# Two batches turned by the tensor engine, products read from PSUM, and a mixer half that no longer shares its time with attention

## The chip, the cores and the metric

The kernel runs on one core of a Trainium2 chip. The metric is device time in microseconds (us). Five engines work side by side, each through its own instructions in order: TensorE (PE; PEld is its weight load), VectorE (DVE), ScalarE (ACT), GpSimd (POOL), and SyncE (SP), which here issues all DMAs from one queue. A step starts when its inputs have come and the buffer it writes is free. TensorE writes to PSUM; DVE and ACT read PSUM, POOL does not.

## The reference

```python
# q, k, v, f_logit: (4, 8, 768, 48); U (768, 32), V (32, 768), w_ch1 (384, 1536), w_ch2 (1536, 384)
f = 1.0 / (1.0 + np.exp(-f_logit))
for t in range(S):                       # gated linear attention, per batch and head
    state = f[:, :, t, :, None] * state + np.einsum('bhd,bhe->bhde', k[:, :, t], v[:, :, t])
    y[:, :, t] = np.einsum('bhd,bhde->bhe', q[:, :, t], state)
x = y.transpose(0, 2, 1, 3).reshape(4, 768, 384)
h = x.transpose(0, 2, 1) @ U @ V         # low-rank mixing over the sequence
u = x + h.transpose(0, 2, 1)
out = u + np.maximum(u @ w_ch1, 0.0) @ w_ch2
```

All data are f32 on the chip; the weights come as f64 and are turned into f32 there.

## The kernel before

Attention works in 16 units of two heads, four to a batch, numbered 0 to 15. Each batch's mixer follows its attention. Two generators give a unit's pieces. `prepare(n)` makes the operands: `gates` (f to channel-major form, sigmoid), `keep` (a backward scan X, L353), `keys` (k times X), `read` (a forward scan Y, L370), `queries` (q times Y, and then the loads of unit n+2 are issued). `attend(n)` has `kept` (k back to token-major form), `scores` for each half of the six 128-token chunks with a causal mask (L406), `states` (products in `ds`, L426, then a short scan of states `st`, L432 and L437), and `read` (40 matmuls with the states, 48 with the masked scores `A`, into `y`). A loop over units writes `prepare(n + 1)` between the pieces of `attend(n)`.

There are two ways to channel-major form. Batch 0 is loaded token-major, in rows of 48 floats (192 bytes), and TensorE transposes it into PSUM (`pt`, L321); ACT copies k and q out, and POOL multiplies them (L336). The other batches are loaded as overlapping runs of 1136 floats for each of 32 rows, and DVE transposes them in blocks (L302); POOL multiplies too.

The mixer of a batch (`mixer_pieces`) has a first part, `low_rank` (`ph`), `mix` (`pu`, added to x by DVE) and `turn` (`put`, copied to `uT` by ACT). Then for each half of the sequence come 12 `ch1` pieces (`pz`, L147, each with a relu `z` on ACT) and 3 `ch2` pieces (`po`, L156, added to x and stored). A piece of `ch1` needs one third of a column block of w_ch1; each `ch2` piece needs all of w_ch2 and all 12 `z`. `pz`, `po`, `pu`, `put`, `ph` and `ds` share two PSUM buffers; `pt`, `sc` and `y` share three others.

`Fill` spreads the mixer pieces of a batch over the 40 slots of the next batch's attention, by cost; the last three `ch2` pieces of a batch are put around the first part of the next mixer. `ahead_by(2, weights)` makes 27 calls, one for each piece of weight, each of which issues a load two pieces ahead and turns the loaded piece into f32: two steps on ACT (L57, L58), three on DVE (L59 to L61), one on POOL (L62). The raw pieces have three buffers, the intermediate ones two. The first 15 pieces (U, V, w_ch1) are spread over batch 0's attention, the 12 of w_ch2 over batch 0's mixer part.

The order on each engine is set by a scheduler that weighs these pieces; the rows of the order are therefore shown with the change.

Of the kernel before, what the change touches and what calls it, by code (L numbers as in the profile page):

```python
# [9 lines left out]
F32 = mybir.dt.float32  # L10
U32 = mybir.dt.uint32
U64 = mybir.dt.uint64
# [4 lines left out]

WP = 384
PAD = 64

# [7 lines left out]
def weight_loader(nc, pool, dma):  # L28
# [8 lines left out]
    def load(dst, w):  # L37
# [4 lines left out]
        T = {}  # L42

        def start():
            raw = T["raw"] = pool.tile([P, WP], U64, name="w_raw", bufs=3)[0:rows, 0:n]
            if len(dst.shape) == 3:
                raw = raw.rearrange("p (c n) -> p c n", c=dst.shape[1])
            dma.dma_start(out=raw, in_=w)
# [58 lines left out]
def mixer_pieces(nc, b, x, U, V, w1, w2, ident, out, two, three, zp, ps_mm):  # L107
# [11 lines left out]
    def low_rank():  # L119
        pm = ps_mm.tile([P, 512], F32, name="ph", tag="mm")  # L120

        for c in range(NCH):
            g = slice((c % NG) * R, (c % NG + 1) * R)
            nc.tensor.matmul(pm[g, 0:DM], lhsT=U[:, c, :], rhs=x[:, c, :],  # L124
                             start=(c < NG), stop=(c >= NCH - NG))
        h[0] = two.tile([P, DM], F32, name="h")
        nc.scalar.copy(h[0], pm[:, 0:DM])
# [46 lines left out]
def factored_path(ctx, tc, q, k, v, f_logit, moe_U, moe_V, moe_w_ch1, moe_w_ch2, out, ok):  # L174
# [20 lines left out]
    HC = C // 2  # L195

    assert S % (2 * C) == 0 and H % 2 == 0 and NB < D <= PAD and PAD == 2 * NB and S % NB == 0
    assert DM % P == 0 and FF % P == 0 and FF % WP == 0 and DM == WP and DM <= 512 and R % 32 == 0 and P % R == 0 and P // R <= NCH
# [24 lines left out]
    def load_unit(n):  # L223
        b, hp = divmod(n, HP)
        for nm in "fkq":
            if b == 0:
                for par in range(2):
                    nc.sync.dma_start(
                        out=nat[n % 2][nm][:, :, par, 0:D],
                        in_=src[nm][b, 2 * hp + par].rearrange("(c p) d -> p c d", p=C),  # L230
                    )
                continue
# [35 lines left out]
    nc.vector.memset(ends, 0.0)  # L268
    nc.vector.memset(ends.rearrange("p (c t) -> p c t", t=C)[:, :, C - 1], 1.0)
    fz = [const.tile([P, S + 1], F32, name=f"fz{i}") for i in range(2)]  # L270
    starts = [const.tile([P, S], F32, name=f"starts{i}") for i in range(2)]
    for i in range(2):
        nc.gpsimd.memset(fz[i], 0.0)
        nc.gpsimd.memset(starts[i], 0.0)
    least = const.tile([P, NU, NCH], F32, name="least")
# [33 lines left out]
    def prepare(n):  # L309
# [3 lines left out]
        b = n // HP  # L313
        r, f, e = raw[n % 2], fz[n % 2], starts[n % 2]
        by_chunk = f[:, 0:S].rearrange("p (c t) -> p c t", t=C)
# [14 lines left out]
        def operand(nm, of):  # L330
            t = T[nm] = two.tile([P, S], F32, name=f"{nm}T")
            if b == 0:
                nc.scalar.copy(halves(t), on_tensor(nm))
            else:
                turned(t, r[nm])
            nc.gpsimd.tensor_tensor(t, t, T[of], ALU.mult)  # L336

        def gates():
            f0 = T["f0"] = two.tile([P, NCH], F32, name="f0")
            if b == 0:  # L340
                pt = on_tensor("f")
                nc.scalar.activation(halves(f)[:, :, :, 1:C], pt[:, :, :, 1:C], AF.Sigmoid)
                nc.scalar.activation(f0.rearrange("p (a c) -> p a c", a=2), pt[:, :, :, 0], AF.Sigmoid)
                return
# [6 lines left out]
        def keep():  # L351
# [5 lines left out]
            X0 = X.rearrange("p (c t) -> p c t", t=C)[:, :, 0]  # L357
            nc.vector.tensor_copy(least[:, n, :], X0)
            X1 = two.tile([P, NCH], F32, name="X1")
            nc.vector.tensor_single_scalar(X1, X0, LEAST, ALU.max)  # L360
            nc.vector.reciprocal(e.rearrange("p (c t) -> p c t", t=C)[:, :, 0], X1)
            whole = T["whole"] = two.tile([P, NCH], F32, name="whole")
# [5 lines left out]
        def read():  # L368
            Y = T["Y"] = one.tile([P, S], F32, name="Y")
            nc.vector.tensor_tensor_scan(Y, f[:, 0:S], e, 0.0, ALU.mult, ALU.add)  # L370

# [12 lines left out]
    def attend(n):  # L384
# [7 lines left out]
        def scores(g):  # L392
# [4 lines left out]
            for c in range(G):  # L397
                for par in range(2):
# [5 lines left out]
                    )  # L404
            for par in range(2):
                nc.vector.tensor_tensor(  # L406
                    T["A"][:, par, g * G : (g + 1) * G, :],
                    sc[:, par, 0 : G * C].rearrange("p (c i) -> p c i", i=C),
                    causal.unsqueeze(1).broadcast_to((P, G, C)),
                    ALU.mult,  # L410
                )

# [64 lines left out]
    load_unit(1)  # L477
    loads = ahead_by(2, weights)
    todo = [(1, f) for f in loads[:first]]
    for piece in prepare(0):  # L480
        piece()
    after = []
    for b in range(B):
# [13 lines left out]
        if b == 0:  # L497

            todo = before + main[0:NFC]
            for i, f in enumerate(loads[first:]):  # L500
                todo.insert(2 * i + 1, (0, f))
            todo += main[NFC:]
        else:

            after[1:1] = before[0:1]
            after[3:3] = before[1 : 1 + NCH]
            after += before[1 + NCH :]
            for _, piece in after:
                piece()
            todo = main  # L510
# [13 lines left out]
def general_path(ctx, tc, q, k, v, f_logit, moe_U, moe_V, moe_w_ch1, moe_w_ch2, out):  # L524
# [249 lines left out]
    for n in range(NSLOT):  # L774
        load_unit(n)
    todo = [(1, f) for f in ahead_by(2, weights)]
    for b in range(B):
# [64 lines left out]
```

## Time and profile before

| | us |
|---|---|
| median of 3 runs (lowest, highest) | 609.67 (608.62, 609.72) |
| the profiled execution: its time, its span | 609.27, 607.5 |
| PE busy | 549.9 (91%) |
| DVE busy | 266.6 (44%) |
| ACT busy, POOL busy | 127.5 (21%), 93.6 (15%) |

The span is the time from the first to the last instruction; the rest of the time, 1.8 us, lies around it. Busy shares are means over the whole span and hide that the stages differ. Matmuls overlap, so a busy PE may still be working at the lower of its two clock levels. An f32 matmul shows as two instructions in the profile.

### The profile page before, as it was taken

Reading aid. Unit: us, or ns where it says so; the run is one execution under the profiler, and the core shown is the slowest. Engines: PE = TensorE matmul, PEld = TensorE weight load, DVE = VectorE, ACT = ScalarE, POOL = GpSimd, SP = SyncE. Lnnn points to the kernel's source line nnn. Section 1 sums busy time; section 2 is a strip of 40 time slices with the busy share of each in tenths; the row PEclk is TensorE's granted clock in tenths of the full one; section 3 lists DMA queues with packets and bytes.
Section 4 is the critical chain, followed back from the end, with each engine's and each line's share of the span. In section 5 each row is a group of like instructions: output and inputs, shape, how many; then the busy total and the mean of one; then the engine's idle time right before and its main releaser. Section 6 shows DMA issues by size and latency. Waiting matters only on the chain.

```text
span 607.5 us, 8789 instructions
## 1 busy us (share of the span) xinstructions
PE 549.9 (91%) x3665; PEld 337.1 (55%) x3665; DVE 266.6 (44%) x411; ACT 127.5 (21%) x252; POOL 93.6 (15%) x76
## 2 busy tenths in 40 slices
PE   4876889767689999999999999999999999999995
PEld 3666446434246655666556655666566555555553
DVE  5799738777845655154845633145122020000000
ACT  4243134224303110321112201220021103200200
POOL 5344022405321220011302110020100000000000
PEclk9677679786979999999899999999999999999998
DMA  9884608814869210502455122010000000000000
GB/s 169 161 158 108 173 0 195 211 39 123 210 145 203 78 34 13 129 19 63 100 129 135 29 67 79 1 21 14 14 14 1 14 13 15 0 13 27 1 15 30
DMA packets 58784, 45.01 MB, mean 74 GB/s; under 512 B 47726, under 2 KB 50798, under 8 KB 58734
## 3 DMA queue, kind: packets, MB, share of 16 engines
q1 hardware_dynamic: 58734, 44.35, 31.3%
q8 instruction: 31, 0.51, 0.3%
q14 instruction: 19, 0.16, 0.1%
HBM read 39.62 MB, written 4.72 MB: 73 GB/s over the span
## 4 chain that ended last, share of the span: by engine, by line
PE 77%; DVE 11%; DMA 6%; ACT 2%; issue 2%; POOL 1%; SPq 0%; DVEq 0%; POOLq 0%; ACTq 0%
PE pz L147 30%; PE po L156 30%; PE y L463 4%; PE sc L399 4%; PE pu L131 3%; DMA w_raw<-in_moe_w_ch_dram 2%; DMA k_raw<-in_k_dram 2%; PE y L454 2%; DVE Y L370 2%; DVE X L353 2%; PE put L140 1%; PE ds L426 1%; DVE A L406 1%; PE ph L124 1%; DVE fT L302 1%
## 5 line engine op out<-in xcount | busy, mean ns | idle before, releaser
L156 PE MATMUL po<-w,z 128*128 128x384 f32 x576 | 198.1, 500 | 10.2 <-POOL w L62 10.2
L147 PE MATMUL pz<-uT,w 128*128 128x384 f32 x576 | 200.7, 501 | 1.2 <-POOL w L62 0.7
L156 PEld LDWEIGHTS po<-w,z 128*128 128x128 f32 x576 | 109.5, 194 | 90.1 <-POOL w L62 15.4
L147 PEld LDWEIGHTS pz<-uT,w 128*128 128x128 f32 x576 | 107.9, 193 | 73.7 <-issue 3.1
L159 DVE TENSOR_TENSOR o<-x,po 128x384 f32<-128x384 f32 x24 | 13.3, 554 | 192.2 <-PE po L156 192.2
L150 ACT ACTIVATE z<-pz 128x384 f32<-128x384 f32 x96 | 47.2, 491 | 215.9 <-PE pz L147 215.9
L336 POOL TENSOR_TENSOR kT<-kT,X 128x768 f32<-128x768 f32 x16 | 29.2, 1823 | 244.4 <-DVE kT L302 234.8
L406 DVE TENSOR_TENSOR A<-sc,causal 128x384 f32<-128x384 f32 x64 | 33.2, 550 | 56.8 <-PE sc L399 56.7
L399 PE MATMUL sc<-qT,kT 48*128 48x128 f32 x384 | 39.1, 310 | 5.3 <-POOL qT L336 5.3
L353 DVE TENSOR_TENSOR_SCAN X<-fz,ends 128x768 f32<-128x768 f32 x16 | 28.6, 1788 | 32.2 <-ACT f L349 10.9
L399 PEld LDWEIGHTS sc<-qT,kT 48*128 48x128 f32 x384 | 29.7, 202 | 21.0 <-issue 13.6
L336 POOL TENSOR_TENSOR qT<-qT,Y 128x768 f32<-128x768 f32 x16 | 31.8, 1988 | 37.1 <-DVE X L360 15.6
L370 DVE TENSOR_TENSOR_SCAN Y<-fz,starts 128x768 f32<-128x768 f32 x16 | 29.5, 1841 | 7.5 <-POOL qT L336 6.8
L62 POOL TENSOR_TENSOR w<-w_y,w_r 128x384 int32<-128x384 int32 x24 | 25.3, 1052 | 46.3 <-DVE w_y L61 41.8
L463 PE MATMUL y<-v_nat,A 128*64 128x48 f32 x768 | 30.2, 242 | 0.0
L454 PE MATMUL y<-st,qT 48*64 48x48 f32 x640 | 18.4, 240 | 12.5 <-DVE st L432 6.8
L463 PEld LDWEIGHTS y<-v_nat,A 128*64 128x64 f32 x768 | 27.9, 157 | 1.3 <-DVE w_y L61 0.3
L454 PEld LDWEIGHTS y<-st,qT 48*64 48x64 f32 x640 | 14.3, 143 | 21.5 <-DVE st L437 8.0
L302 DVE STREAM_TRANSPOSE fT<-f_raw 128x768 f32<-128x768 f32 x12 | 25.0, 2080 | 0.4 <-DMA f_raw<-in_f_logit_dram 0.3
L302 DVE STREAM_TRANSPOSE qT<-q_raw 128x768 f32<-128x768 f32 x12 | 25.1, 2088 | 0.0
L302 DVE STREAM_TRANSPOSE kT<-k_raw 128x768 f32<-128x768 f32 x12 | 24.9, 2073 | 0.0
L131 PE MATMUL pu<-h,V 128*128 128x384 f32 x48 | 21.3, 560 | 1.6 <-DVE x L132 1.1
(61 smaller groups left out, 305.2 us busy)
## 6 DMA issues: line engine op xcount, KB each, us to landing
w_raw<-in_moe_w_ch_dram SPq DMA_DIRECT2D x24, 384.0 KB, 3.5
f_raw<-in_f_logit_dram SPq DMA_DIRECT2D x47, 142.0 KB, 3.4
k_raw<-in_k_dram SPq DMA_DIRECT2D x47, 142.0 KB, 3.5
q_raw<-in_q_dram SPq DMA_DIRECT2D x47, 142.0 KB, 5.1
v_nat<-in_v_dram SPq DMA_DIRECT2D x32, 144.0 KB, 3.5
out_dram<-o SPq DMA_DIRECT2D x24, 192.0 KB, 1.9
f_raw<-in_f_logit_dram SPq DMA_DIRECT2D x8, 144.0 KB, 10.2
k_raw<-in_k_dram SPq DMA_DIRECT2D x8, 144.0 KB, 8.8
```

What stands on the lines that cost most here:

```text
L131: nc.tensor.matmul(pm[:, 0:DM], lhsT=V[:, t * P : (t + 1) * P], rhs=h[0], start=True, stop=True)
L147: nc.tensor.matmul(pm[:, 0:HALF], lhsT=w1[:, m, i * P : (i + 1) * P], rhs=uT[a][:, m, :], start=(m == 0), stop=(m == NDC - 1))
L150: nc.scalar.activation(z[a, i], pm[:, 0:HALF], AF.Relu)
L156: nc.tensor.matmul(pm[:, 0:DM], lhsT=z[a, i][:, s * P : (s + 1) * P], rhs=w2[:, i, :], start=(i == 0), stop=(i == NFC - 1))
L302: nc.vector.transpose(t.rearrange("p (i c) -> p c i", c=TB), bass.AP(src_tile.tensor, src_tile.offset, [list(src_tile.ap[0]), [D, TB], [1, ...
L336: nc.gpsimd.tensor_tensor(t, t, T[of], ALU.mult)
L353: nc.vector.tensor_tensor_scan(backwards(X, S - 1, S), backwards(f, S, S), backwards(ends, S - 1, S), 0.0, ALU.mult, ALU.add,)
L370: nc.vector.tensor_tensor_scan(Y, f[:, 0:S], e, 0.0, ALU.mult, ALU.add)
L399: nc.tensor.matmul(sc[:, par, c * C : (c + 1) * C], lhsT=T["k"][rows[par], chunk[g * G + c]], rhs=T["q"][rows[par], chunk[g * G + c]], sta ...
L406: nc.vector.tensor_tensor(T["A"][:, par, g * G : (g + 1) * G, :], sc[:, par, 0 : G * C].rearrange("p (c i) -> p c i", i=C), causal.unsquee ...
L454: nc.tensor.matmul(o(a, par, c), lhsT=T["q"][rows[par], c * C + a * HC : c * C + (a + 1) * HC], rhs=T["st"][rows[par], c - 1, :], start=(c ...
L463: nc.tensor.matmul(o(a, par, c), lhsT=T["A"][:, par, c, halves[a]], rhs=vt[:, c, par, :], start=False, stop=True, skip_group_check=True,)
```

## The change

Batches 0 and 1 (`TURNED = 2`) are now loaded token-major and turned by TensorE. For them DVE multiplies straight out of PSUM, which replaces the ACT copy and the POOL product. The causal mask is applied to both heads by one DVE instruction instead of two. A copy of six columns (`least`) moves from DVE to ACT. `starts` has one buffer instead of two. Raw weights have four buffers and are loaded three ahead. Only the first 8 pieces of weight are turned in batch 0's attention. The other 19 go beside the first part of batch 0's mixer and its first 12 `ch1` pieces, which are all written out before batch 1's attention and no longer spread over it.

```diff
-            raw = T["raw"] = pool.tile([P, WP], U64, name="w_raw", bufs=3)[0:rows, 0:n]
+            raw = T["raw"] = pool.tile([P, WP], U64, name="w_raw", bufs=RAW)[0:rows, 0:n]
...
+    TURNED = 2
...
-            if b == 0:
+            if b < TURNED:
                 for par in range(2):
                     nc.sync.dma_start(
...
-            if b == 0:
-                nc.scalar.copy(halves(t), on_tensor(nm))
+            if b < TURNED:
+                nc.vector.tensor_tensor(halves(t), on_tensor(nm), halves(T[of]), ALU.mult)
             else:
                 turned(t, r[nm])
-            nc.gpsimd.tensor_tensor(t, t, T[of], ALU.mult)
+                nc.gpsimd.tensor_tensor(t, t, T[of], ALU.mult)
...
-            nc.vector.tensor_copy(least[:, n, :], X0)
+            nc.scalar.copy(least[:, n, :], X0)
...
-            for par in range(2):
-                nc.vector.tensor_tensor(
-                    T["A"][:, par, g * G : (g + 1) * G, :],
...
+            nc.vector.tensor_tensor(
+                T["A"][:, :, g * G : (g + 1) * G, :],
...
-    loads = ahead_by(2, weights)
-    todo = [(1, f) for f in loads[:first]]
+    loads = ahead_by(RAW - 1, weights)
+
+    early = first - 7
+    todo = [(1, f) for f in loads[:early]]
+    loads = loads[early:]
...
-            todo = before + main[0:NFC]
-            for i, f in enumerate(loads[first:]):
-                todo.insert(2 * i + 1, (0, f))
-            todo += main[NFC:]
+            for i, (_, piece) in enumerate(before + main[0:NFC]):
+                if loads and (i % 2 == 0 or i >= len(before)):
+                    loads.pop(0)()
+                piece()
+            for f in loads:
+                f()
+            todo = main[NFC:]
```

Three places of the order matter later. Line numbers of the changed kernel are up to 10 higher.

DVE in batch 0's attention, from the scan of one unit to the last work before the next scan. Before:

```order
L353 SCALAR_TENSOR_TENSOR X<-fz_113,ends 128x768
L358 COPY least<-X 128x6
L360 TENSOR_SCALAR X_600<-X 128x6
L363 TENSOR_TENSOR whole<-f_564,X 128x6
L361 RECIPROCAL starts_115<-X_600 128x6
L370 SCALAR_TENSOR_TENSOR Y<-fz_113,starts_115 128x768
L406 TENSOR_TENSOR A<-sc,causal 128x384 x2
L432 TENSOR_TENSOR st<-ds,whole 128x240
```

The same stretch in the changed kernel:

```order
L358 SCALAR_TENSOR_TENSOR X<-fz_114,ends 128x768
L365 TENSOR_SCALAR X_384<-X 128x6
L368 TENSOR_TENSOR whole<-f_348,X 128x6
L338 TENSOR_TENSOR kT<-pt,X 128x768
L366 RECIPROCAL starts<-X_384 128x6
L375 SCALAR_TENSOR_TENSOR Y<-fz_114,starts 128x768
L410 TENSOR_TENSOR A<-sc,causal 128x2x384
L436 TENSOR_TENSOR st<-ds,whole 128x240
```

The product of k now stands between the two scans on DVE (that of q follows later), and one wide mask stands for two.

PE from the last matmuls of unit 3 (`y`) through batch 0's mixer. Before, where `sc`, `ds` and `y` after the first `pz` are unit 4's:

```order
L463 MATMUL y<-v_nat,A 64x48 x24
L124 MATMUL ph<-x,U 32x384 x6
L131 MATMUL pu<-h,V 128x384 x6
L140 MATMUL put<-ident,x 128x128 x8
L418 MATMUL pt<-ident,kT 128x64 x10
L140 MATMUL put<-ident,x 128x128 x10
L147 MATMUL pz<-uT,w_123 128x384 x7
L399 MATMUL sc<-qT,kT 128x128 x6
L147 MATMUL pz<-uT,w_123 128x384 x2
L426 MATMUL ds<-v_nat,kb 64x48 x10
```

In the changed kernel, from the last `put` on:

```order
L142 MATMUL put<-ident,x 128x128 x3
L149 MATMUL pz<-uT,w_121 128x384 x36
L158 MATMUL po<-w_122,z 128x384 x12
L430 MATMUL ds<-v_nat,kb 64x48 x10
L326 MATMUL pt<-ident,q_raw_85 128x128
L404 MATMUL sc<-qT,kT 128x128 x6
L158 MATMUL po<-w_122,z 128x384 x12
L458 MATMUL y<-st,qT 64x48 x20
L467 MATMUL y<-v_nat,A 64x48 x24
```

All 12 `ch1` pieces of the first half and one `ch2` piece now stand ahead of unit 4's `ds`.

ACT beside those `pz`, in the changed kernel (w_y and w_r are the two ACT steps of a piece of weight):

```order
L144 COPY uT<-put 128x3x128 x6
L152 ACTIVATE z<-pz 128x384
L59 ACTIVATE w_y<-w_raw 128x384
L60 ACTIVATE w_r<-w_raw 128x384
L59 ACTIVATE w_y<-w_raw 128x384
L60 ACTIVATE w_r<-w_raw 128x384
L152 ACTIVATE z<-pz 128x384
L59 ACTIVATE w_y<-w_raw 128x384
L60 ACTIVATE w_r<-w_raw 128x384
```

In this manner 16 pieces of weight stand between the 12 relus, one or two to a relu; the last two relus follow the last piece. Before, the first 6 relus had four pieces between them, and then the sigmoid of a unit followed.

## Rows read from the trace of the kernel before

**Rows 1.** Windows, five stages: us, busy (instructions) by engine, PEclk, DMA share, GB/s.

```profile
0.00:66.46 66.46, 45.11 (x640) 37.97 (x641) 53.68 (x91) 24.21 (x45) 29.20 (x34) 0.80 0.85 156
66.46:83.65 17.19, 13.65 (x52) 6.30 (x53) 10.82 (x14) 4.16 (x9) 3.63 (x2) 0.70 0.24 78
83.65:181.50 97.85, 74.88 (x474) 43.03 (x473) 65.52 (x105) 29.07 (x59) 28.36 (x23) 0.84 0.57 142
181.50:213.75 32.25, 32.25 (x306) 20.33 (x303) 18.56 (x25) 8.04 (x16) 5.49 (x3) 1.00 0.61 137
213.75:607.50 393.75, 384.05 (x2203) 229.52 (x2199) 118.02 (x176) 61.98 (x124) 26.94 (x14) 0.99 0.14 38
```

**Rows 2.** Waits of the SP queue: line waited for, us in total, times, longest.

```profile
SPq L48 <- DVE w_y L61: 79.2, 17, 27.7
```

**Rows 3.** Timeline, DVE: scans of units 2 and 3; start, us, idle before.

```profile
29.79 1.76 DVE L353 TENSOR_TENSOR_SCAN X<-fz,ends 128x768 f32<-128x768 f32 x1 [3.58 <-ACT f L343]
...
44.63 2.26 DVE L353 TENSOR_TENSOR_SCAN X<-fz,ends 128x768 f32<-128x768 f32 x1 [0.49 <-ACT fz L342]
```

**Rows 4.** Timeline, unit 3: a POOL product and the forward scan.

```profile
47.06 1.86 POOL L336 TENSOR_TENSOR kT<-kT,X 128x768 f32<-128x768 f32 x1 [1.78 <-DVE X L353]
...
47.43 3.10 DVE L370 TENSOR_TENSOR_SCAN Y<-fz,starts 128x768 f32<-128x768 f32 x1
```

**Rows 5.** Groups by line and form: busy us, mean ns; idle before and releasers.

```profile
L406 DVE TENSOR_TENSOR A<-sc,causal 128x384 f32<-128x384 f32 x64 | 33.2, 550 | 56.8 <-PE sc L399 56.7
...
L353 DVE TENSOR_TENSOR_SCAN X<-fz,ends 128x768 f32<-128x768 f32 x16 | 28.6, 1788 | 32.2 <-ACT f L349 10.9 <-POOL kT L336 8.1 <-ACT fz L342 5.5
...
L437 DVE SCALAR_TENSOR_TENSOR st<-st,whole 128x48 f32<-128x48 f32 x64 | 19.6, 306 | 1.8
L61 DVE SCALAR_TENSOR_TENSOR w_y<-w_raw,w_y 128x384 uint32<-128x384 uint32 x26 | 17.0, 654 | 0.6
L60 DVE TENSOR_SCALAR w_y<-w_y 128x384 uint32<-128x384 uint32 x26 | 13.4, 514 | 0.4
...
L59 DVE TENSOR_SCALAR w_y<-w_y 128x384 f32<-128x384 f32 x26 | 12.2, 467 | 6.7 <-ACT w_y L57 6.7
...
L432 DVE TENSOR_TENSOR st<-ds,whole 128x240 f32<-128x240 f32 x16 | 6.4, 403 | 23.9 <-PE ds L426 23.9
```

**Rows 6.** Windows of loading: mostly 192-byte rows; mostly runs of 4.5 KB.

```profile
10.00:18.00 8.00, 4.18 (x48) 3.47 (x50) 7.83 (x9) 2.26 (x4) 5.62 (x3) 0.90 1.24 166
97.00:105.00 8.00, 8.00 (x108) 5.25 (x108) 5.66 (x12) 3.31 (x7) 2.00 (x2) 1.00 1.09 225
```

**Rows 7.** Timeline, PE: the first three `pu` of batch 0.

```profile
69.81 4.21 PE L131 MATMUL pu<-h,V 128*128 128x384 f32 x6 [0.58 <-ACT h L127]
```

**Rows 8.** Timeline, PE: six transposes of f.

```profile
10.44 0.85 PE L321 MATMUL pt<-ident,f_raw 128*128 128x128 f32 x6 [1.40 <-DMA f_raw<-in_f_logit_dram]
```

**Rows 9.** Timeline, POOL: last step of three pieces of weight in a row.

```profile
152.89 1.00 POOL L62 TENSOR_TENSOR w<-w_y,w_r 128x384 int32<-128x384 int32 x1 [0.95 <-DVE w_y L61]
155.24 0.99 POOL L62 TENSOR_TENSOR w<-w_y,w_r 128x384 int32<-128x384 int32 x1 [1.35 <-ACT w_r L58]
157.18 0.99 POOL L62 TENSOR_TENSOR w<-w_y,w_r 128x384 int32<-128x384 int32 x1 [0.95 <-DVE w_y L61]
```

**Rows 10.** Chain that ended last, pieces between 180 and 222 us: start, us.

```profile
180.85 0.72 PE ds L426 x20
...
185.63 0.73 PE y L454 x40
186.36 1.54 PE y L463 x48
...
198.42 0.87 PE sc L399 x12
...
213.82 7.94 PE po L156 x24
```

**Rows 11.** Timeline, PE: a burst of `po` that waits for weights.

```profile
158.23 1.56 PE L156 MATMUL po<-w,z 128*128 128x384 f32 x4 [0.39 <-POOL w L62]
```

More of the change, by code (lines that the diff above doesn't have):

```diff
@@ L18 @@
 WP = 384
+RAW = 4
 PAD = 64
@@ L125, in low_rank @@
                              start=(c < NG), stop=(c >= NCH - NG))
-        h[0] = two.tile([P, DM], F32, name="h")
+        h[0] = two.tile([P, DM], F32, name="h", bufs=1)
         nc.scalar.copy(h[0], pm[:, 0:DM])
@@ L269, in factored_path @@
     nc.vector.memset(ends.rearrange("p (c t) -> p c t", t=C)[:, :, C - 1], 1.0)
+    starts = const.tile([P, S], F32, name="starts")
+    nc.gpsimd.memset(starts, 0.0)
     fz = [const.tile([P, S + 1], F32, name=f"fz{i}") for i in range(2)]
-    starts = [const.tile([P, S], F32, name=f"starts{i}") for i in range(2)]
     for i in range(2):
         nc.gpsimd.memset(fz[i], 0.0)
-        nc.gpsimd.memset(starts[i], 0.0)
     least = const.tile([P, NU, NCH], F32, name="least")
@@ L313, in prepare @@
         b = n // HP
-        r, f, e = raw[n % 2], fz[n % 2], starts[n % 2]
+        r, f = raw[n % 2], fz[n % 2]
         by_chunk = f[:, 0:S].rearrange("p (c t) -> p c t", t=C)
@@ L331, in operand @@
             t = T[nm] = two.tile([P, S], F32, name=f"{nm}T")
-            if b == 0:
-                nc.scalar.copy(halves(t), on_tensor(nm))
+            if b < TURNED:
+                nc.vector.tensor_tensor(halves(t), on_tensor(nm), halves(T[of]), ALU.mult)
             else:
                 turned(t, r[nm])
-            nc.gpsimd.tensor_tensor(t, t, T[of], ALU.mult)
+                nc.gpsimd.tensor_tensor(t, t, T[of], ALU.mult)
         def gates():
             f0 = T["f0"] = two.tile([P, NCH], F32, name="f0")
-            if b == 0:
+            if b < TURNED:
                 pt = on_tensor("f")
@@ L357, in keep @@
             X0 = X.rearrange("p (c t) -> p c t", t=C)[:, :, 0]
-            nc.vector.tensor_copy(least[:, n, :], X0)
+            nc.scalar.copy(least[:, n, :], X0)
             X1 = two.tile([P, NCH], F32, name="X1")
             nc.vector.tensor_single_scalar(X1, X0, LEAST, ALU.max)
-            nc.vector.reciprocal(e.rearrange("p (c t) -> p c t", t=C)[:, :, 0], X1)
+            nc.vector.reciprocal(starts.rearrange("p (c t) -> p c t", t=C)[:, :, 0], X1)
             whole = T["whole"] = two.tile([P, NCH], F32, name="whole")
@@ L369, in read @@
             Y = T["Y"] = one.tile([P, S], F32, name="Y")
-            nc.vector.tensor_tensor_scan(Y, f[:, 0:S], e, 0.0, ALU.mult, ALU.add)
+            nc.vector.tensor_tensor_scan(Y, f[:, 0:S], starts, 0.0, ALU.mult, ALU.add)
         def queries():
@@ L404, in scores @@
                     )
-            for par in range(2):
-                nc.vector.tensor_tensor(
-                    T["A"][:, par, g * G : (g + 1) * G, :],
[L408 to L411, printed above, removed]
+            nc.vector.tensor_tensor(
+                T["A"][:, :, g * G : (g + 1) * G, :],
+                sc[:, :, 0 : G * C].rearrange("p h (c i) -> p h c i", i=C),
+                causal.unsqueeze(1).unsqueeze(1).broadcast_to((P, 2, G, C)),
+                ALU.mult,
+            )
         def kept():
@@ L775, in general_path @@
         load_unit(n)
-    todo = [(1, f) for f in ahead_by(2, weights)]
+    todo = [(1, f) for f in ahead_by(RAW - 1, weights)]
     for b in range(B):
```

## The prediction

> **What bounds the kernel now.** I read the windows by stage first [rows 1]. From 213.75 us to the end TensorE is busy 384.05 of 393.75 us at a granted clock of 0.99: that stage, 65% of the span, is TensorE's, with batches 2 and 3 under the mixer's products. The 32.25 us before it are also full, at 1.00. The loss is all ahead of 181.5 us. Batch 0's attention (66.46 us) has TensorE busy 45.11 us at 0.80, and DVE busy 53.68 us: DVE sets the pace there. The mixer's first part takes 17.19 us at 0.70. Then come 97.85 us in which no engine is full: PE is busy 74.88 us at 0.84, with waits between. Second, the scans of units 2 and 3 give the pace of batch 0: 44.63 less 29.79 is 14.84 us a unit [rows 3]. Third, the waits of the SP queue: it stood 79.2 us, once for 27.7 us, on a load of weights whose raw buffer DVE had not yet read [rows 2]; the loads of batch 1's units stand behind it in that one queue, so their attention and the products that need late weights both start late.
>
> So I work out one number: when TensorE reaches the piece that started at 213.75 us (the first `ch2` piece of batch 0's second half). Behind it the change moves nothing but small DVE work under a full TensorE, and I add the same 393.75 us.
>
> **Batch 0's attention, unit for unit.** Added on DVE: two products from PSUM per unit. No row shows one of 768 columns. The two PSUM rows, 403 ns for 240 columns and 550 ns for 384, lie on a line of 1.02 ns a column, which puts 768 at 0.94 us [rows 5]; twice 550 ns is the upper bound, 0.55 the lower; I take 0.95, so 1.9 us a unit. Two wide masks at the same 0.95 for four at 0.55 give back 0.3 us. `least` on ACT gives back 0.2 us or so; ACT has room (24.21 of 66.46 us busy [rows 1]). Removed: two POOL products of 1.86 us a unit. They cost DVE time too: the forward scan of unit 3 took 3.10 us, started 0.4 us into one, against 1.79 us as the mean of the other scan [rows 4, 5]. That is up to 1.3 us a stall, for two products a unit. Half the weights leave this stage; a piece costs DVE 0.467 + 0.514 + 0.654 = 1.64 us [rows 5]. The sum for a unit in the changed kernel is two scans 3.6, products 1.9, masks 1.9, states 0.40 + 4 x 0.31 = 1.6, small columns 0.6, two pieces of weight 3.3: 12.9 us. Waiting comes on top. The products hold their `pt` buffers longer, and the f transposes of the next unit still stand behind q's product or behind `y`, which needs the last mask; DVE waited 3.58 and 0.49 us there before [rows 3], and I take 2.3 us a unit. That makes 15.2 us: no faster than before.
>
> But the stage now does more. Unit 4 is fully prepared in it, where before its loads were late and its scan came after batch 0's end. From 29.8 us, three such steps put the scan of unit 5 at 75.4 us, and unit 3's last `y` and the start of `ph` at about 75 us, where it was 66.46: plus 8.5. The bounds are DVE's plain sum, 7 us of start and loading and 4.7 units of 12.9 us, which gives 67, and a wait of 3.58 us in each unit, 79.
>
> **The loads of units 4 to 7.** A unit's f, k, q and v in 192-byte rows is 8 x 144 KB; this form moved at 166 GB/s in a window of almost nothing else, so 7.1 us a unit. The old form moved at 225 GB/s, but with 12 x 142 KB for f, k and q plus v's two, 2.0 MB, so 9 us [rows 6]. I count no cost: DMA work per unit shrinks. By the Trainium skill (DMA: Bandwidth & Descriptors, Why small descriptors are slow) small descriptors are the slow ones, which speaks against this edit. The rate in this trace agrees, 166 against 225 GB/s; the bytes, which the rule does not count, turn it round. By the rule alone, at equal bytes, a unit would cost 12 us.
>
> **The mixer's first part.** The 17.19 us had waits for POOL products and DVE transposes of unit 4, which fall away. Added are 11 transposes for unit 5 (0.85 us for six [rows 8]) and six score products. Early `pu` stay slow, 0.70 us each [rows 7]. I keep 17 us, so `pz` starts at 92 (bounds 84 and 96, from the stage ahead).
>
> **The weights beside the products.** Sixteen of the 19 late pieces stand on ACT between the 12 relus, and the last `ch2` input is there only when they are through. TensorE's own work here, 24 us for 72 `pz`, is the shorter chain. The first relu comes 3.5 us after the first `pz`, at 95.5. Pieces in a row came 2.35 and 1.94 us apart before [rows 9]; the longer step waited for a load, which four buffers should cure, but each second piece now waits behind a relu of 0.5 us. I take 2.15 us: 16 x 2.15 = 34.4, so ACT is free for the last relus at 130 us, and the first `ch2` piece runs from there, 7.94 us [rows 10], to 138. Bounds: 1.94 and 2.35 a piece, 31 and 38 us.
>
> **Batch 1's attention under the rest.** What is left to the mark is the full window of 32.25 us [rows 1] plus what stood ahead of it before: two `ch2` pieces 15.9, three `ds` 2.2, two `y` of 2.27 each 4.5, five half scores 4.4, two `kept` 0.9 (an estimate, 20 small transposes), 37 transposes at 0.14 us [rows 8, 10], 5.2: 65.3 us. In all the change adds 72 transposes to TensorE; at 0.14 us each 10 us of its work are their price, where before DVE had them, and they are counted here and in the two stages ahead. The chains of units 5 to 7 are started early and the `ch2` pieces cover them, so I add 1.2 us of waits. The mark is at 138 + 66.5 = 204.5 us, against 213.75: 9.25 us earlier.
>
> **The sum.** 204.5 + 393.75 = 598.25 us of span; with the 1.8 us around it the profiled execution would be 600.0. Its 609.27 stands 0.4 under the median, which I leave. Three runs of before lie within 0.18%, so 0.2% (1.2 us) is about what can be told from no change.
>
> **Rivals.**
>
> *DVE's waits go too.* If PSUM products take the POOL stall out and the f transposes cease to be late, batch 0's attention ends at 67 us, not 75, and the gain is 17 us: 592. With weights at 1.94 us it is 588. For it: the 3.10 us scan. Against it: of the 14.84 us between two scans, the waits were at the f transposes, which stand where they stood.
>
> *TensorE falls to 1.2 GHz beside the weights (slower).* It is asked for 24 us of work in 34. If its clock stays low, a `pz` piece costs 4.2 us (six at 0.70 [rows 7]), the relus wait for it in ACT's order and hold the weights up: 12 x 4.2 = 50 us in place of 38 from 92 to 130, and the `ch2` piece doubles to 16. That adds 20 us, 620; it decides the sign once more than half of the stretch is slow. For it: the stage from 83.65 to 181.5 us was granted 0.84 only. Against it: bursts of four `po` that waited between weights took 1.56 us, 0.39 each, the fast rate [rows 11].
>
> *Given back under batch 1.* If units 5, 6 and 7 have their scan, product, `kept`, score chain open, with only 47 us of mixer under them where before there were 94, each leaves TensorE 2 to 4 us idle (a scan and a product of 2.7 us): 6 to 12 us, 606 to 612.
>
> *Loads late.* At equal bytes the four units' loads would add 3 us each to a DMA that is 0.85 busy in batch 0 [rows 1]; two of them fall before 75 us: 606.
>
> **How the numbers follow.** My forecast, 593 to 607, gets 0.50 around 600. The DVE case, 584 to 593, gets 0.22; the slow clock, 611 to 622, 0.15; given back, 606 to 612, 0.08; late loads, 604 to 609, 0.05. The range that leaves out no more than 2 in 10 is 585 to 613; it holds the bounds of 1.94 and 2.35 us a weight and of 67 and 79 us for batch 0. Faster by over 0.2% (under 608.4) is the forecast, the DVE case and part of the last two, 0.77; the slow clock and the far end of the given-back case are slower, 0.17; 0.06 is left for no change.
>
> **What would show it.** Right: scans still 15 us apart in batch 0 and no POOL work but weights in the first 130 us; `ph` near 75 us; weight steps on POOL 2.0 to 2.3 us apart beside `pz`; the first `po` near 130, with relus waited for by PE; then TensorE full to the end, and an SP queue that no longer stands 27.7 us on a weight. Wrong: `ph` at 67 (DVE case), `pz` at 0.64 us or more each (clock), idle PE between `po` and `sc` of units 5 to 7 (given back), or a stage behind the mark that is not 394 us long, which I have taken over unchanged.

## The result, and the profile after

The changed kernel takes 591.17 us (median of 4 runs, 590.63 to 592.01). The kernel before took 609.14 us beside it. The ratio is 0.9713, with a 95% interval of 0.9683 to 0.9744. The profiled execution took 590.83 us with a span of 589.1. The forecast was 600.0 us in a range of 585 to 613, so the sign and the range held, but the gain was twice the size: 18.4 us of span in place of 9.25. (The change also gives `h`, the result of `low_rank`, one buffer instead of two, which its description leaves out.)

Windows of the changed kernel, cut where the steps of the prediction are cut (`ph`, `pz`, `po` begin; the `ch2` pieces of the second half begin). The columns are those of [rows 1].

```profile
0.00:69.39 69.39, 55.02 (x669) 45.64 (x669) 49.12 (x93) 20.24 (x44) 12.71 (x25) 0.69 0.96 176
69.39:82.41 13.02, 12.21 (x73) 7.08 (x72) 10.96 (x19) 5.81 (x14) 2.00 (x2) 0.97 0.51 142
82.41:114.96 32.55, 24.51 (x73) 13.03 (x73) 28.30 (x47) 20.78 (x45) 14.51 (x15) 1.00 0.63 163
114.96:122.87 7.91, 7.91 (x25) 4.45 (x25) 1.18 (x2) 0.23 (x1) 1.39 (x2) 1.00 0.01 3
122.87:190.07 67.20, 65.56 (x704) 43.81 (x704) 45.96 (x61) 13.57 (x30) 6.06 (x3) 1.00 0.43 105
190.07:589.10 399.03, 385.41 (x2203) 230.21 (x2199) 109.27 (x147) 61.13 (x128) 25.75 (x14) 0.99 0.14 38
```

| stage | predicted, us | after, us | difference |
|---|---|---|---|
| batch 0's attention, to `ph` | 75 | 69.39 | -5.6 |
| first mixer part, to `pz` | 17 | 13.02 | -4.0 |
| first products and weights, to `po` | 38 | 32.55 | -5.5 |
| first `ch2` piece | 8 | 7.91 | -0.1 |
| rest of batch 1, to the mark | 66.5 | 67.20 | +0.7 |
| behind the mark | 393.75 | 399.03 | +5.3 |

The mark is reached at 190.07 us, where it was 213.75: 23.7 us earlier, not 9.25. But the stage behind it, which I carried over unchanged, lost 5.28 us. TensorE's idle time there grew from 9.70 us [rows 1] to 13.62 (399.03 less 385.41), and its busy time by 1.36 us.

Two waits, 6.67 us together, are more than that growth. Behind the first, 24 products took 9.70 us; 24 like them take 8.01 us at other places of this stage. The timeline of TensorE, where the waits end (the value in brackets is the idle time and what ended it):

```profile
256.83 9.70 PE L158 MATMUL po<-w,z 128*128 128x384 f32 x24 [1.96 <-ACT z L152]
...
309.46 3.66 PE L149 MATMUL pz<-uT,w 128*128 128x384 f32 x6 [4.71 <-ACT z L152]
```

And ACT's timeline at the same two places. L353 is the sigmoid that `gates` issues for a unit turned by DVE.

```profile
255.56 0.84 ACT L353 ACTIVATE fz<-fT 128x762 f32<-128x762 f32 x1 [4.69 <-DVE Y L375]
256.30 0.47 ACT L152 ACTIVATE z<-pz 128x384 f32<-128x384 f32 x1
...
308.19 0.84 ACT L353 ACTIVATE fz<-fT 128x762 f32<-128x762 f32 x1 [6.56 <-DVE fT L307]
308.93 0.47 ACT L152 ACTIVATE z<-pz 128x384 f32<-128x384 f32 x1
```

The relu that TensorE waits for had its `pz` by 254.0 and 304.7 us. It stands on ACT behind a sigmoid that waits for DVE. The sigmoids are those of units 13 and 15, and the scans that read them start only at 298.70 and 386.31 us. The loads of weights, which had held SP for 79.2 us [rows 2], now hold it for less than half of that (total, times, longest):

```profile
SPq L50 <- DVE w_y L63: 32.6, 14, 7.8
```

### The profile page after: what moved, and what is told of

The parts are those of the page before. It is cut to its first block, busy times and chain, and to the rows that moved or that the text cites. A ratio compares the mean times of both kernels' runs of the same rounds, so it can differ in the third digit from the quotient of the medians.

```text
span 589.1 us, 8824 instructions
## 1 busy us (share of the span) xinstructions
PE 550.6 (93%) x3737; PEld 344.2 (58%) x3737; DVE 244.8 (42%) x367; ACT 121.8 (21%) x260; POOL 62.4 (11%) x59
## 4 chain that ended last, share of the span: by engine, by line
PE 80%; DVE 11%; DMA 3%; SPq 2%; ACT 1%; issue 1%; POOL 0%; DVEq 0%; ACTq 0%; POOLq 0%
PE po L158 32%; PE pz L149 26%; PE sc L404 5%; PE y L467 4%; PE pu L133 3%; PE pt L326 3%; DVE w_y L62 2%; DMA w_raw<-in_moe_V_dram 2%; PE y L458 2%; PE ds L430 2%; PE put L142 2%; DVE w_y L63 1%; SPq L232 1%; DVE X L358 1%; DVE Y L375 1%
## 5 line engine op out<-in xcount | busy, mean ns | idle before, releaser
L158 PE MATMUL po<-w,z 128*128 128x384 f32 x576 | 192.2, 492 | 3.7 <-ACT z L152 3.7
L149 PEld LDWEIGHTS pz<-uT,w 128*128 128x128 f32 x576 | 106.3, 191 | 85.7 <-ACT z L152 12.9
L410 DVE TENSOR_TENSOR A<-sc,causal 128x768 f32<-128x768 f32 x32 | 30.3, 947 | 63.2 <-PE sc L404 63.2
L341 POOL TENSOR_TENSOR kT<-kT,X 128x768 f32<-128x768 f32 x8 | 14.6, 1820 | 243.4 <-DVE kT L307 243.4
L473 ACT COPY x<-y 128x576 f32<-128x576 f32 x16 | 10.2, 636 | 61.2 <-PE y L467 61.2
L144 ACT COPY uT<-put 128x384 f32<-128x384 f32 x24 | 10.7, 480 | 53.7 <-PE put L142 53.7
L62 DVE TENSOR_SCALAR w_y<-w_y 128x384 uint32<-128x384 uint32 (+1 forms) x27 | 20.3, 752 | 0.7
L133 PE MATMUL pu<-h,V 128*128 128x384 f32 x48 | 19.4, 514 | 0.8 <-DVE x L134 0.8
L341 POOL TENSOR_TENSOR qT<-qT,Y 128x768 f32<-128x768 f32 x8 | 17.2, 2156 | 17.8 <-DVE X L365 11.7
```

Of the source, the lines that this page charges most:

```text
L62: nc.vector.tensor_scalar(y, y, 3, 0x3FFFFFFF, ALU.logical_shift_left, ALU.bitwise_and)
L133: nc.tensor.matmul(pm[:, 0:DM], lhsT=V[:, t * P : (t + 1) * P], rhs=h[0], start=True, stop=True)
L149: nc.tensor.matmul(pm[:, 0:HALF], lhsT=w1[:, m, i * P : (i + 1) * P], rhs=uT[a][:, m, :], start=(m == 0), stop=(m == NDC - 1))
L158: nc.tensor.matmul(pm[:, 0:DM], lhsT=z[a, i][:, s * P : (s + 1) * P], rhs=w2[:, i, :], start=(i == 0), stop=(i == NFC - 1))
L410: nc.vector.tensor_tensor(T["A"][:, :, g * G : (g + 1) * G, :], sc[:, :, 0 : G * C].rearrange("p h (c i) -> p h c i", i=C), causal.unsquee ...
```

## The experiments

Ratios are to the kernel before, run beside each. Its own median moved from 609.1 to 611.2 us from one set of runs to the next, so times of different sets are compared to some 2 us at best, and ratios by their intervals.

| kernel | median, us | ratio (95%) |
|---|---|---|
| changed kernel | 591.17 | 0.9713 (0.9683 to 0.9744) |
| order alone, on the kernel before | 608.81 | 0.9995 (0.9974 to 1.0016) |
| batch 1 turned by DVE | 607.90 | 0.9973 (0.9955 to 0.9990) |
| old order | 594.49 | 0.9759 (0.9716 to 0.9802) |
| products on POOL | 592.46 | 0.9723 (0.9701 to 0.9746) |
| 12 pieces early, `least` on DVE | 591.67 | 0.9704 (0.9672 to 0.9735) |
| three raw buffers | 588.73 | 0.9630 (0.9598 to 0.9662) |
| masks apart | 586.86 | 0.9610 (0.9579 to 0.9642) |
| `least` on DVE | 586.01 | 0.9614 (0.9594 to 0.9634) |
| the same, two-tensor shift | 586.59 | 0.9609 (0.9580 to 0.9639) |
| the same, and DVE products later | 585.58 | 0.9595 (0.9566 to 0.9624) |
| `least` on DVE, DVE products later | 584.33 | 0.9582 (0.9550 to 0.9614) |
| `least` on DVE, OR in place of POOL's sum | 579.71 | 0.9500 (0.9461 to 0.9539) |

The profiled executions tell more than the medians, since they can be cut at the mark. Each row is one execution:

| kernel | mark, us | behind the mark, us |
|---|---|---|
| before | 213.75 | 393.75 |
| order alone | 208.87 | 397.6 |
| batch 1 turned by DVE | 206.93 | 397.0 |
| old order | 188.50 | 403.5 |
| changed kernel | 190.07 | 399.03 |

**The order alone, on the kernel before.** The blocks of the change's diff that concern weights and their order, with one buffer for `starts` and for `h` as in the change.

> The kernel before with one part of the change: weights in four raw buffers, 8 pieces in batch 0's attention and 19 beside the first mixer part and the first 12 products, one starts buffer. Batch 1 still turned by DVE, products still on POOL, masks apart. Theory A (the parts need each other: units 4 to 7 still need three DVE transposes of 2.1 us and two POOL products of 1.8 us each, and these stand in line with the weights' 16 pieces on DVE and POOL): little or no gain, 600 to 610 us, weight steps on POOL above 2.2 us apart. Theory B (the order alone brings the gain, by keeping 7 pieces of 1.64 us out of batch 0 and the mixer half together): 590 to 597 us, weight steps at 1.95 us, first po before 120 us.

Nothing was gained in all, as theory A said. Batch 0's attention did end earlier (`ph` at 63.98 us), but the first `po` came at 134.85, later than before (126.08). The mark came 4.9 us earlier, and 3.9 of them were lost behind it, where TensorE waits 4.78 us for a relu.

**Batch 1 turned by DVE.**

```diff
-    TURNED = 2
+    TURNED = 1
```

> The changed kernel, batch 1 turned by DVE again (three transposes of 2.1 us and two POOL products of 1.8 us a unit, loads in 4.5 KB runs). Theory A: batch 0's attention ends earlier than 69.4 us by up to 3 us because the f of unit 5 is not turned there, but the weights' stage from the first pz to the first po, 32.6 us, grows to 40 us or more, and the time is 597 to 604 us. Theory B (TensorE pays as much for the 72 transposes, some 10 us, as DVE is spared): 588 to 593 us.

Worse than theory A: 607.9 us, nearly all of the gain gone. The edit also takes back batch 1's products on DVE, which the run with products on POOL shows to be worth little, and its loads in 192-byte rows, which were not tried apart (the share of DMA in the window below is 0.37). Its window from the first `pz` to the first `po` lasts 53.75 us, 21 us more than in the changed kernel, with no engine full:

```profile
79.94:133.69 53.75, 31.64 (x98) 16.70 (x97) 45.28 (x57) 20.82 (x46) 18.79 (x17) 0.78 0.37 105
```

The timeline of one stretch in it, ACT, DVE and TensorE:

```profile
94.45 0.53 ACT L60 ACTIVATE w_r<-w_raw 128x384 int32<-128x384 uint32 x1
107.63 0.84 ACT L353 ACTIVATE fz<-fT 128x762 f32<-128x762 f32 x1 [12.64 <-DVE fT L307]
...
101.21 1.84 DVE L62 TENSOR_SCALAR w_y<-w_y 128x384 uint32<-128x384 uint32 x1
...
105.51 2.08 DVE L307 STREAM_TRANSPOSE fT<-f_raw 128x768 f32<-128x768 f32 x1
...
104.84 1.65 PE L149 MATMUL pz<-uT,w 128*128 128x384 f32 x2 [11.48 <-POOL w L64]
```

ACT, which opens each piece of weight, stands for 12.64 us at the sigmoid of the next unit. That waits for a transpose on DVE, which stands there from 95.20 us on behind two masks, two transposes and two pieces of weight, one of them held up by a POOL product. Meanwhile TensorE waits 11.48 us for a column block of w_ch1. The kernel with the order alone has the same wait at the same place, 13.38 us. When TensorE turns batch 1, as in the changed kernel, its transposes stand in TensorE's own order behind the `pz`, so no unit is prepared between the weights: DVE scans no X between 69.92 and 136.67 us. That is what was bought for 72 transposes of TensorE.

**The old order, the rest as changed.** The order blocks of the diff undone.

> The changed kernel with the weights and the mixer half in the old order: 15 pieces in batch 0's attention, 12 beside the mixer, the first mixer part and the first 12 products spread over batch 1's attention again. Everything else as changed. The order alone on the kernel before was worth nothing (ratio 0.9995), batch 1 turned by DVE cost 16.7 us in the changed kernel. Theory C (the two parts need each other: only with both is a stage free for the weights): 600 to 607 us. Theory D (turning batch 1 on TensorE carries the gain alone, with any order): 588 to 594 us.

594.49 us, at the edge of theory D: about four fifths of the gain comes with the old order too, once batch 1 is turned by TensorE. The 0.5% between the two is not clear of the scatter, since the intervals overlap. Nor does it come from the weights' stage: the mark is 1.6 us earlier with the old order (188.50 us), and what is lost lies behind it, with two waits for relus of 4.9 us each.

**Products on POOL.**

```diff
-                nc.vector.tensor_tensor(halves(t), on_tensor(nm), halves(T[of]), ALU.mult)
+                nc.scalar.copy(halves(t), on_tensor(nm))
             else:
                 turned(t, r[nm])
-                nc.gpsimd.tensor_tensor(t, t, T[of], ALU.mult)
+            nc.gpsimd.tensor_tensor(t, t, T[of], ALU.mult)
```

> The changed kernel, with ACT copying k and q of batches 0 and 1 out of PSUM and POOL multiplying them, as before. Theory A (the POOL product blocks DVE, as the 3.10 us scan showed, and that is what my 15.2 us a unit kept in and the chip did not show): the scans of units 1 to 4 again 14 to 16 us apart, ph at 74 to 77 us in place of 69.4, the time 596 to 600 us. Theory B (the unit got shorter because half of the weights left batch 0, and the products are worth little): ph within 2 us of 69.4, the time 590 to 593 us.

Theory B: the time is within the interval of the changed kernel's, and `ph` is 2.1 us from it. The stall is real, but it was absorbed: a forward scan beside a POOL product took 2.88 us again, `ph` came at 67.26 us, `pz` at 85.72 (18.46 us later, at a granted clock of 0.78), and the first `po` at 114.69 us, where it was 114.96. The time lost ahead of `pz` came back because the relus stand earlier among the weights on ACT: four of POOL's sums start behind the first `po` there, and one in the changed kernel.

**`least` on DVE.**

```diff
-            nc.scalar.copy(least[:, n, :], X0)
+            nc.vector.tensor_copy(least[:, n, :], X0)
```

> The changed kernel with the copy of six columns on DVE again. The stage behind the mark is 399.0 us in the changed kernel and was 393.75 before. Theory L (the copy, which stands on ACT and waits there 32.5 us for the scans X, holds the relus up): the stage is 394 to 395 us, the time 586 to 587 us. Theory S (the sigmoids of units 13 and 15, which stand on ACT ahead of a relu and wait for DVE, hold them up, and their place does not move with this edit): the two waits of PE, 2.0 and 4.7 us, stay, the stage is 398 to 399.5 us, the time 590 to 592 us.

Each theory was half right. The time is theory L's, 586.01 us. But both waits behind the mark stay, as theory S said (here and below such a row can count only the products up to the end of its view):

```profile
252.26 4.19 PE L158 MATMUL po<-w,z 128*128 128x384 f32 x8 [2.02 <-ACT z L152]
304.88 1.65 PE L149 MATMUL pz<-uT,w 128*128 128x384 f32 x2 [4.71 <-ACT z L152]
```

The 4.4 us of span were won ahead of the mark: `ph` 0.6 us earlier; 32.55 us from `pz` to `po` became 30.58, since of the last two relus, which stood behind the last piece of weight on ACT, one now stands ahead of it; and a TensorE wait of 1.64 us at 176.4 us is gone. Of that one the copy was the cause. In the changed kernel's ACT timeline the relu follows the copy, which waits for a scan:

```profile
175.77 0.20 ACT L363 COPY least<-X 128x6 f32<-128x6 f32 x1 [1.88 <-DVE X L358]
175.88 0.48 ACT L152 ACTIVATE z<-pz 128x384 f32<-128x384 f32 x1
```

The next five start from this kernel.

**The OR.** POOL's integer sum gives way to a DVE operation; the carry into a weight's last place is left out.

```diff
-            nc.scalar.activation(r, lo, AF.Copy, scale=2.0**-29)
+            nc.scalar.activation(r, lo, AF.Copy, scale=2.0**-29, bias=-0.5)
-            nc.gpsimd.tensor_tensor(flat.bitcast(I32), y.bitcast(I32), r, ALU.add)
+            nc.vector.tensor_tensor(flat.bitcast(I32), y.bitcast(I32), r, ALU.bitwise_or)
```

> The changed kernel with the copy of six columns on DVE again (586.0 us), and the last step of a weight, POOL's integer addition, replaced by an OR on DVE of a rounded-down number; the carry into the last place is left out, so some weights differ in their last bits. Theory P (the 1.95 us between weights are DVE's three steps, of which the second is held up by POOL's addition, 1.05 us in place of 0.35): steps of 1.6 to 1.75 us, from the first pz to the first po 27 us in place of 30.6, time 582 to 583.5 us. Theory Q (ACT's two steps and its relus set the distance, or TensorE's waits for relus do): steps of 1.9 us or more, time 585 to 587 us.

Theory P, and 2 us better than it said. The window from the first `pz` to the first `po`, and DVE in it:

```profile
81.11:105.97 24.86, 23.86 (x72) 13.62 (x73) 23.56 (x59) 18.93 (x42) 0.00 (x0) 1.00 0.74 214
```

```profile
98.36 0.55 DVE L64 TENSOR_TENSOR w<-w_y,w_r 128x384 int32<-128x384 int32 x1
98.83 0.35 DVE L62 TENSOR_SCALAR w_y<-w_y 128x384 uint32<-128x384 uint32 x1
99.21 0.56 DVE L63 SCALAR_TENSOR_TENSOR w_y<-w_raw,w_y 128x384 uint32<-128x384 uint32 x1
99.69 0.35 DVE L61 TENSOR_SCALAR w_y<-w_y 128x384 f32<-128x384 f32 x1
99.96 0.55 DVE L64 TENSOR_TENSOR w<-w_y,w_r 128x384 int32<-128x384 int32 x1
```

Steps are 1.60 us with four operations on DVE, against 1.95 with three and POOL beside them. TensorE is busy for 23.86 of 24.86 us: the weights no longer set the stage.

**The two-tensor shift.** A tile holds the mask.

```diff
-            nc.vector.tensor_scalar(y, y, 3, 0x3FFFFFFF, ALU.logical_shift_left, ALU.bitwise_and)
+            nc.vector.scalar_tensor_tensor(y, y, 3, low30[0:rows, 0:n].bitcast(U32),
+                                           ALU.logical_shift_left, ALU.bitwise_and)
```

> The changed kernel with the copy of six columns on DVE again (586.0 us), and the shift of a weight as an instruction with two tensors (shift by 3, then AND with a tile that holds the mask) in place of one with two constants; POOL's addition stays, and the result is the same to the bit. Theory P (only the form with one tensor is held up by POOL: 1.05 us beside it and 0.35 alone, while the form with two tensors took 0.55 in either case): steps of 1.45 to 1.6 us beside the products, no wait of TensorE for a relu between the first pz and the first po, 25 us between them, time 578.5 to 582 us as with the OR. Theory R (the OR's gain came from POOL having no part, whichever step POOL holds up): the two-tensor form is held up as well, steps of 1.9 us or more, time 585 to 587 us.

Theory R. DVE's timeline, the first shift without POOL, the second beside its sum (0.99 us from 86.96):

```profile
85.66 0.56 DVE L64 SCALAR_TENSOR_TENSOR w_y<-w_y,low 128x384 uint32<-128x384 uint32 x1
...
87.12 1.25 DVE L64 SCALAR_TENSOR_TENSOR w_y<-w_y,low 128x384 uint32<-128x384 uint32 x1
```

This form is held up by 0.7 us too, and the step grew to 2.15. The Trainium skill (SBUF — State Buffer, Who interferes with whom) has it: a DVE instruction with two SBUF inputs contends with a GpSimd instruction that reads SBUF, and one in a 2-port mode contends with GpSimd as well. The trace agrees on the first, 1.25 against 0.56 us here. The old form is held up too, 1.05 against 0.36 us; whether it ran in such a mode no run shows.

**12 pieces early.** `early = first - 3`.

> The changed kernel with the copy of six columns on DVE again (586.0 us), and 12 pieces of weight in batch 0's attention, 15 beside the first mixer part and the first products (8 and 19 in the changed kernel). Theory I (DVE waited 3.7, 1.3 and 3.5 us ahead of the scans of units 3 to 5 for f transposes, so four pieces of 1.26 us fit in there, and the weights' stage loses four steps of 1.95 us): ph within 2 us of 68.8, first po at 106 to 109 us, time 581 to 584 us. Theory J (DVE sets the pace of batch 0, and each piece moved there delays it as much): ph at 73 to 75 us, time 585 to 588 us.

Theory J, and more: `ph` at 75.59 us, 6.8 us later for four pieces, and the weights' stage only 1.7 us shorter (28.91 us). So a piece moved there costs batch 0 1.7 us and gives back 0.4 us behind it. TensorE is busy for 24.04 of the 28.91 us, and the other 4.87 are mostly the waits for three relus, which still stand among the weights.

**DVE products behind batch 1.**

```diff
-                nc.gpsimd.tensor_tensor(t, t, T[of], ALU.mult)
+                nc.vector.tensor_tensor(t, t, T[of], ALU.mult)
```

> The changed kernel with the copy of six columns on DVE again (586.0 us), and the products of batches 2 and 3 on DVE in place of POOL; the order on ACT is the same as without this edit. Theory T (the chain on DVE, whose scans wait 2.0 and 1.7 us for POOL's products, makes the fT and Y late that the sigmoids wait for, and the relus behind them): the waits of PE of 2.0 and 4.7 us behind the mark fall to under 0.5 and 3 us, time 580.5 to 583.5 us. Theory U (the sigmoid's place alone sets it, ahead of a relu that TensorE needs): both waits stay within 1 us, time 585 to 587 us.

In between. ACT's order is the same, and the waits shrink, the second by 2.1 us:

```profile
252.41 2.31 PE L158 MATMUL po<-w,z 128*128 128x384 f32 x4 [1.74 <-ACT z L152]
302.96 2.30 PE L149 MATMUL pz<-uT,w 128*128 128x384 f32 x5 [2.63 <-ACT z L152]
```

So the place of the sigmoid makes the wait, and the DVE chain ahead of it sets a part of its length. The time, 584.33 us, is not clear of the 586.01 us without the edit, since the intervals overlap.

**Both, with the two-tensor shift.**

> The last kernel with the products of batches 2 and 3 on DVE as well. If the two edits act in different stages they add: 1.5 to 2 us under the last kernel, 577 to 580 us; if the relus behind the mark are held up by the sigmoids' place alone, within 1 us of it.

585.58 us, 1 us under the two-tensor shift alone, inside the scatter of both (584.7 to 587.3 and 586.3 to 589.1); inconclusive.

**Three raw buffers**, on the changed kernel: `RAW = 3`.

> The changed kernel with three raw buffers and loads two ahead, as before. My step: four buffers keep a weight's step from waiting for a load, 2.15 us in place of 2.35. Theory P of the steps (DVE under POOL's lock sets 1.95 us, loads are there in time): steps 1.95 us, time 590 to 592 us. Theory M (the fourth buffer is what made the steps even): each second step 2.3 us or more, first po 3 to 6 us later, time 594 to 597 us.

Theory M for the steps, neither for the time. In the first half of the stage POOL's timeline shows steps of 2.0 and 2.35 us in turn, as in [rows 9]:

```profile
92.25 1.06 POOL L64 TENSOR_TENSOR w<-w_y,w_r 128x384 int32<-128x384 int32 x1 [1.35 <-DVE w_y L63]
94.27 1.00 POOL L64 TENSOR_TENSOR w<-w_y,w_r 128x384 int32<-128x384 int32 x1 [0.95 <-DVE w_y L63]
96.62 1.07 POOL L64 TENSOR_TENSOR w<-w_y,w_r 128x384 int32<-128x384 int32 x1 [1.35 <-DVE w_y L63]
```

Yet the first `po` came at 113.90 us, because more pieces were put ahead of the first relu. The fourth buffer evens the steps and bought no time: the kernel with three is even faster, 0.9630 against 0.9713, and the intervals do not meet. Its profiled execution was the slowest of the four (591.37 us), so where that time lies is not shown.

**Masks apart**, on the changed kernel: two instructions of 384 columns for each half.

> The changed kernel with the causal mask as two instructions of 384 columns a half again. My step: two wide masks at 0.95 us for four at 0.55 us, 0.3 us a unit on DVE; four units ahead of ph, so ph 1 to 1.5 us later, and 1 us in the time, 591.5 to 593 us. Rival: DVE's waits of 3.7, 1.3 and 3.5 us for f transposes take it up, ph within 0.5 us of 69.4 and the time within 0.6 us of 591.2.

`ph` came 0.8 us later, a little less than my step said, but the time fell to 586.86 us. Its profile shows where: the first `po` is 1 us earlier (30.8 us behind `pz`, since relus stand earlier on ACT), and 3 us are won behind the mark. There the second wait is 3.04 us and not 4.71. The first is the same, 2.03 us, but the 24 products after it took 8.01 us and not 9.70. Windows behind that wait, first the changed kernel, then this one; PEclk is the third value from the end:

```profile
257.50:266.00 8.50, 8.50 (x22) 4.76 (x21) 0.00 (x0) 0.24 (x1) 0.00 (x0) 0.80 0.00 0
```

```profile
256.00:265.00 9.00, 9.00 (x50) 5.49 (x52) 0.79 (x2) 0.92 (x2) 0.00 (x0) 1.00 0.00 0
```

So the wide mask gives DVE about what I counted, and what it lost elsewhere is order on ACT, the length of a wait and clock after a wait, which the edit does not aim at.

## Why the prediction was right in sign and half the size

The mark came 14.4 us earlier than forecast, and 5.3 us of that were given back behind it. Without this second error the time would have stood at the lower end of the range, so the total is nearer than its parts by luck.

**Batch 0's attention, 75 us: mis-sized, and its pace misread.** The DVE scans of units 2 to 5 in the changed kernel are 13.7 us apart on average, not 15.2:

```profile
28.73 1.76 DVE L358 TENSOR_TENSOR_SCAN X<-fz,ends 128x768 f32<-128x768 f32 x1 [1.50 <-ACT fz L347]
...
43.94 1.76 DVE L358 TENSOR_TENSOR_SCAN X<-fz,ends 128x768 f32<-128x768 f32 x1 [3.67 <-ACT fz L347]
...
55.77 1.76 DVE L358 TENSOR_TENSOR_SCAN X<-fz,ends 128x768 f32<-128x768 f32 x1 [1.33 <-ACT fz L347]
...
69.92 1.76 DVE L358 TENSOR_TENSOR_SCAN X<-fz,ends 128x768 f32<-128x768 f32 x1 [3.50 <-ACT fz L347]
```

The waits did not go, so the rival that said so was wrong in its mechanism though its time was the nearest: they are 2.8 us on average, where I took 2.3. The error is in DVE's own work. The windows of one such step before, and of the three steps in the changed kernel, show 13.96 us of it before and 10.5 us on average after, where I had 12.9:

```profile
29.79:44.63 14.84, 11.12 (x164) 9.51 (x163) 13.96 (x24) 6.41 (x13) 5.97 (x5) 0.76 0.89 158
```

```profile
28.73:43.94 15.21, 15.21 (x186) 12.95 (x183) 10.62 (x21) 4.95 (x12) 2.00 (x2) 0.54 1.15 228
43.94:55.77 11.83, 9.67 (x142) 7.81 (x142) 10.39 (x21) 3.46 (x9) 1.99 (x2) 0.74 1.10 196
55.77:69.92 14.15, 12.34 (x180) 9.65 (x180) 10.52 (x20) 4.69 (x11) 1.99 (x2) 0.74 0.80 153
```

I had taken means [rows 5] that contain POOL's stalls: a piece of weight is 0.35, 0.35 and 0.55 us without one, 1.25 and not 1.64, which is 0.8 us for two. About half of the error is that I added up durations: the rows of successive DVE instructions overlap, mostly by some 0.1 us, and the 20 rows of a step add up to 11.8 us.

So before, DVE was nearly full and set the pace, as I had it. In the changed kernel it does not: TensorE is busy for 37.2 of the 41.2 us of the three steps, at a granted clock of 0.54, 0.74 and 0.74, and DVE for 31.5. The long waits, ahead of the scans of units 3 and 5, are for f transposes four of which stand on TensorE behind all 48 `y` products. Ahead of unit 4's they stand between the two halves of `y`, and the wait is 1.33 us. TensorE's timeline for units 3 and 4:

```profile
39.36 2.80 PE L467 MATMUL y<-v_nat,A 128*64 128x48 f32 x48
42.09 0.97 PE L326 MATMUL pt<-ident,f_raw 128*128 128x128 f32 x4
...
51.90 1.52 PE L467 MATMUL y<-v_nat,A 128*64 128x48 f32 x24
53.35 1.54 PE L326 MATMUL pt<-ident,f_raw 128*128 128x128 f32 x6
54.82 1.52 PE L467 MATMUL y<-v_nat,A 128*64 128x48 f32 x24
```

In the kernel with the OR they stand between the halves in all three steps. DVE has more to do there, 11.6 us a step, but the waits are 0.35, 0.85 and 0.40 us, and the scans are 12.5 us apart. With three raw buffers they stand there too, and the waits are 2.1 to 2.6 us. So the longest waits go with the order that TensorE is given, but that is not all of them, and no run changes it alone. The two kernels with 12 and 15 pieces in this stage have scans 14.8 and 14.6 us apart, so what I called no faster than before is true with the weights of before.

**The first mixer part, 17 us: too long by 4.** I kept it from a stage at a clock of 0.70; it ran at 0.97. Eleven other kernels took 12.7 to 15.8 us, the one with POOL products 18.46 us at 0.78. What holds the clock up there I did not separate.

**The weights, 2.15 us each: too long.** The steps are 1.95 us, my lower bound, which is 3.2 of the 5.5 us for 16 pieces; the first relu, 2.2 us behind the first `pz` and not 3.5, is 1.3. The fourth buffer does cure the longer step, and relus do not lengthen it, because ACT has room beside a step that DVE sets. DVE's second operation, in the changed kernel:

```profile
85.98 0.36 DVE L62 TENSOR_SCALAR w_y<-w_y 128x384 uint32<-128x384 uint32 x1
...
87.24 1.05 DVE L62 TENSOR_SCALAR w_y<-w_y 128x384 uint32<-128x384 uint32 x1
...
89.19 1.05 DVE L62 TENSOR_SCALAR w_y<-w_y 128x384 uint32<-128x384 uint32 x1
```

The OR shows that POOL's sum sets the 1.95. That the weights, not TensorE, bound this stage was right, and the slow clock did not come: 1.00 throughout.

**The rest of batch 1, 66.5 us: right** (67.20), and nothing was given back there. TensorE's one wait in it is the 1.64 us for a relu. For loaded f and k it waited 1.8 us in the whole execution, all ahead of `ph`, so the loads in 192-byte rows cost it no more than that directly.

**Behind the mark, unchanged: wrong.** The step that failed is "behind it the change moves nothing but small DVE work under a full TensorE". The change moved the sigmoids and relus on ACT against each other. All the variants made from the changed kernel or from its order alone show a TensorE wait of 2.6 to 4.9 us behind the mark; the kernel before has none over 0.9. Which edit moves the sigmoid there is not settled, since both the order alone and the old order with the rest have it. Neither `least` on ACT nor the fourth raw buffer is the cause, since the kernels without them have the waits too. What all these kernels share against the kernel before is one buffer for `starts` and for `h`; no run has two again, so this stays a suspicion.

**Small parts counted as gains or as nothing.** `least` on ACT, the wide masks and the fourth raw buffer each cost time as part of this kernel: with one of them undone it takes 586.01, 586.86 and 588.73 us, and none of the three intervals meets that of the changed kernel. What all three undone together would give was not run.

**What carries the gain** I had spread over both stages. It hangs on one edit, batch 1 on TensorE, by a mechanism that I named for the loads only: with DVE turning batch 1, weights and units wait for each other on ACT, DVE and POOL. With the new order this edit moves the mark by 16.9 us (206.93 to 190.07). Once TensorE turns batch 1, the new order no longer brings the mark forward (188.50 us with the old one). The edit by itself on the kernel before was not run.

## What to carry to other kernels

When work for a later stage and urgent work share several in-order engines, ask on each of them what stands ahead of the urgent piece; moving the later stage to an engine that is itself behind the urgent work can be worth more than its cost there. A mean duration that contains another engine's stalls must not be used for a kernel in which that engine is idle, and durations added up can exceed the busy time that a window shows. An engine that was nearly full may stop setting the pace once its work shrinks; look then at what the others are given ahead of its inputs. A full stage carried over unchanged needs its order on the other engines compared as well: a wait of 2 to 5 us on ACT costs its length, and sometimes slow products after it.

## What the runs showed of the hardware

After nearly the same wait of TensorE, 1.96, 2.02, 2.03 and 1.74 us, the clock that was granted to the 24 products behind it was not the same: 0.80 (9.70 us) in the changed kernel and 0.82 with `least` on DVE, a mean over both levels, but 1.00 (8.01 us), the upper level throughout, with the masks apart and in the kernel with both edits. Ten of the profiled kernels have this wait, of 1.74 to 2.03 us; in four of them the products took 9.6 to 9.7 us, in six 8.01. So two executions with the same wait can differ by 1.7 us for this alone. And a DVE instruction beside a POOL sum of 0.99 us was held up by the same 0.7 us, whether it read one tensor or two.
